# Attention scores of two heads in two 64-row halves of TensorE, in one visit a unit around the products with v

## The chip, the core and the metric

The kernel runs on one core of one Trainium2 chip. The core has TensorE (PE; its weight loads are shown apart as PEld), VectorE (DVE), ScalarE (ACT), GpSimd (POOL) and SyncE (SP, here a queue that issues DMAs). TensorE writes to PSUM, which holds eight banks of 512 float32 values for each of its 128 partitions. The metric is the time on the device in microseconds (us), the median of several runs.

## The reference, cut to what matters

The kernel computes a transformer block: an adaptive layer norm, attention with a memory over four segments, its output projection with residual, a second norm, and a gated feed-forward network. The change is in the attention of a segment:

```python
B, S, D, H = 1, 2048, 576, 32
Dh = D // H; N = 4; L = S // N                 # head size 18, four segments of 512 positions
mask = (ar[:, None] < ar[None, :]) * (-1e9)
for s in range(N):
    qs, ks, vs = q[:, :, s], k[:, :, s], v[:, :, s]
    logits = jnp.einsum("bhqd,bhkd->bhqk", qs, ks) * scale + mask
    p = _softmax(logits, axis=-1)
    a_dot = jnp.einsum("bhqk,bhkd->bhqd", p, vs)
    a_mem = num / den                          # from the memory of the segments before
    o = g * a_mem + (1.0 - g) * a_dot
```

## The kernel before

The work goes in stages: the first norm with the projections to q, k and v (to about 227 us), the attention (to about 573 us), the feed-forward network (the rest). q and k lie in DRAM (`qD`, `kD`), split into a high and a low part, so that a product of three parts (high with high, low with high, high with low) has nearly the precision of float32. A head has 18 features, hence 54 rows of such parts.

The attention goes over 32 *units*: four heads of one segment each (`units`, `NU`). The four heads are two pairs (`a`), and a pair lies in one *stack*: 108 rows, 54 for each of its heads (`e`). In `kst` the rows of both heads hold k; in `qst` there is a column block for each head in which the other head's rows are zero, so a product over 108 rows gives one head's scores. Rows 108 and 109 hold ones in `kst` and the negated row maximum, high and low part, in `qst`, so that the products for the softmax (`p2_step`, 110 rows) come with the maximum subtracted. There are `NB` = 4 stacks. At any time unit u is in its scores and products with v, u + 1 waits for its maxima, u + 2 has its row maxima taken, and u + 3 is loaded.

For unit u the loop over steps k does, mixed with one another:
- `p1_step` for unit u + 2: scores of row block i (128 rows of q against the 128(i+1) keys that the mask leaves), in 3 PSUM banks (`S1B`, tag s1), and the maximum of each row by VectorE. Behind block 0 GpSimd splits the maxima into high and low (`mc`).
- event `m` for unit u + 1: TensorE transposes `mc` into `pmt`; event `n`: ScalarE copies it to `mr` (`mt_b`), and `put_m` writes it into the stack by DMA.
- `p2_step` for unit u: scores transposed (key block j against the queries that may see it), in 3 banks (`S2B`, tag s2), the exponential by ScalarE into `Pt`, and the diagonal block cut by GpSimd (`affine_select`).
- `av_step` for unit u - 1: the products of `Pt` with v, four heads in four groups of 32 columns of the array, all at step `BK` = 0, behind the first score product; then `ev_step` copies `av` on ScalarE.
- events `U` and `V`: `load_k` and `load_q` for unit u + 3. Other events are the output projection of the segment before (M, X, R, S, T), the memory terms (A, B, C, D, G), the second norm (l, p, x) and preparations of weights.

The order on every engine is the order of the code (`manual_schedule`): the table `PAT` says at which of the 11 steps of a unit each event stands, by the unit's half of a segment and parity, and `KP`, `RL` and `step_of` place further work by numbers of steps. All loads, `put_m` and stores of this stage are issued by SyncE's queue in that order. An instruction that waits holds up all that stand behind it on its engine.

Of the kernel before, what the change touches and what calls it, by code (L numbers as in the profile page):

```python
# [26 lines left out]
VC = 624  # L27
EPS = 1e-5
# [20 lines left out]
KP = (7, 8, 1, 3)  # L49
# [12 lines left out]
NE = 2  # L62
E1 = 2
E2 = 1
BK = 0
PAT = (["E", "", "m U D", "c", "n V G", "Q d", "M0", "g M1 M2 M3 X", "h A0", "R S q T Y Z B0", "A1 f P z B1 C"],
# [7 lines left out]
RL = (-10, -1, 0, 4, 4, 9, 10, 10, 12, 10, 11, 12, 15, 16)  # L74
SUMS = ((4, 3, 2, ALU.add), (5, 4, 0, ALU.subtract), (3, 0, 3, ALU.subtract), (6, 1, 5, ALU.subtract))
S1B, S2B, XB, WB = 3, 3, 2, 1
# [7 lines left out]
def block(ctx: ExitStack, tc: tile.TileContext, x, wqk, wv, wo, beta, wgu, wgr, wd, c, crow, w_mod, w_mod0, w_mod1, w_modc, xt, out):  # L84
# [58 lines left out]
    def new_stack(b, stk):  # L143
# [5 lines left out]
        nc.gpsimd.memset(f32(qst[b][:, 2:4]), 0.0)  # L149

    def new_ones(b):
        nc.sync.dma_start(f32(kst[b][108:110]).rearrange("p a (b c) -> p (a b) c", c=P),
                          ones[0:2, :].unsqueeze(1).to_broadcast([2, 8, P]))
# [36 lines left out]
    def load_k(u, b):  # L190
        s, q = units[u]
        k = kD[s].rearrange("(Q a f) z t -> Q f z a t", Q=8, a=2)[q]
        ks = f32(kst[b][0:108]).rearrange("(f z) a t -> f z a t", z=3)
        for z in range(3):
            nc.sync.dma_start(ks[:, z], k[:, z // 2])

    def load_q(u, b):
        s, q = units[u]
        v = qD[s].rearrange("f z t -> (f z) t").rearrange("(Q a r) t -> Q r a t", Q=8, a=2)[q]
        for r0, r1 in ((0, 48), (54, 102), (48, 54), (102, 108)):  # L200
            nc.sync.dma_start(f32(qst[b][r0:r1, r0 // 54:4:2, :]), v[r0:r1])

    def put_m(u, b):
        mr = mrow.pop(u)
        for a in range(2):
            nc.sync.dma_start(f32(qst[b][108 + a:109 + a]).rearrange("p a t -> p (a t)"), mr[16 * a:16 * a + 16])

    def p1_step(u, b, i, ps, jp, jb):
        if i == 3:
            mcol[u] = (mwk.tile([P, 4, 4], F32, tag="mx", name="mx"),  # L210
                       mwk.tile([P, 2, 4, 4], F32R, tag="mc", name="mc"))
        mx, mc = mcol[u]
        n = 128 * (i + 1)
        per = L // n if n <= 256 else 1
        for h0 in range(0, 4, per):
            bank = ps.tile([P, L], F32, tag="s1", name="s1", bufs=SB[-1])
# [1614 lines left out]
```

## Time and profile before

| | us |
|---|---|
| median of 3 runs | 1820.09 |
| lowest, highest | 1817.81, 1820.72 |
| profiled execution (its span) | 1819.8 |
| attention, 237.05 to 540.70 us (28 units) | 303.65 |
| TensorE busy in it | 295.98 |
| VectorE busy in it | 253.67 |
| ScalarE busy in it | 241.84 |
| GpSimd busy in it | 204.06 |

The profile gives no time for the profiled execution but its span, from the first to the last instruction. It comes from one execution on the chip. A timeline row has start, duration, engine, line of the kernel, operation, tile written <- tiles read, shape, the number of instructions merged into it, and in brackets the idle time ahead of it with what ended it. "108*128 108x512" is a product over 108 rows with 128 columns of weights and 512 columns streamed. SPq is the queue of SyncE: a row there is the issue of DMAs, not their transfer. Records of matmuls overlap, since they are pipelined, so what one costs is read from start to start.

### The profile page before, as it was taken

Reading aid. Unit: us, or ns where it says so; the run is one execution under the profiler, and the core shown is the slowest. Engines: PE = TensorE matmul, PEld = TensorE weight load, DVE = VectorE, ACT = ScalarE, POOL = GpSimd, SP = SyncE. Lnnn points to the kernel's source line nnn. Section 1 sums busy time; section 2 is a strip of 40 time slices with the busy share of each in tenths; the row PEclk is TensorE's granted clock in tenths of the full one; section 3 lists DMA queues with packets and bytes.
Section 4 is the critical chain, followed back from the end, with each engine's and each line's share of the span. In section 5 each row is a group of like instructions: output and inputs, shape, how many; then the busy total and the mean of one; then the engine's idle time right before and its main releaser. Section 6 shows DMA issues by size and latency. Waiting matters only on the chain.

```text
span 1819.8 us, 31453 instructions
## 1 busy us (share of the span) xinstructions
PE 1791.3 (98%) x10627; PEld 1521.3 (84%) x10627; DVE 1484.4 (82%) x3365; ACT 1086.4 (60%) x2374; POOL 674.9 (37%) x1110
## 2 busy tenths in 40 slices
PE   7999989999999999999999999999999999999999
PEld 4888856777777888888888888888888888888888
DVE  7556378888886899889889889868888888888886
ACT  4334288878776567777777777534544544444542
POOL 3444077775567655656656656300000000000000
PEclk9999999999999999999999999999999999999999
DMA  7768765667657655455455354494233334324331
GB/s 264 265 225 278 263 208 178 214 201 220 172 170 237 202 178 185 135 181 178 134 183 176 115 173 147 158 311 151 101 107 121 98 96 130 104 82 129 107 103 53
DMA packets 146115, 306.26 MB, mean 168 GB/s; under 512 B 30916, under 2 KB 61764, under 8 KB 144164
## 3 DMA queue, kind: packets, MB, share of 16 engines
q1 hardware_dynamic: 134772, 260.19, 46.7%
q10 hardware_dynamic: 11184, 44.07, 6.1%
q8 instruction: 85, 1.39, 0.3%
q14 instruction: 74, 0.61, 0.1%
HBM read 198.69 MB, written 104.94 MB: 167 GB/s over the span
## 4 chain that ended last, share of the span: by engine, by line
PE 93%; DMA 2%; ACT 2%; DVE 1%; issue 1%; POOL 0%; SPq 0%; ACTq 0%; DVEq 0%; POOLq 0%
PE A L1349 25%; PE pd L1468 20%; PE C L1349 13%; PE B L1349 6%; PE pp L113 5%; PE s L218 4%; PE av L745 4%; PE s L721 3%; PE pv L113 3%; PE pw L863 3%; PE pd L1488 3%; ACT Pt L728 1%; PE pn L931 1%; PE pm L550 1%; PE px L766 1%
## 5 line engine op out<-in xcount | busy, mean ns | idle before, releaser
L1349 PE MATMUL A<-y,wh 128*128 128x512 f32 x1152 | 404.1, 391 | 0.7 <-ACT cu L1378 0.7
L1476 DVE TENSOR_TENSOR acc<-acc,pd 128x576 f32<-128x576 f32 x327 | 245.2, 750 | 78.2 <-PE pd L1468 71.9
L1468 PE MATMUL pd<-dh,ah 128*128 128x288 f32 x896 | 267.4, 298 | 0.0
L1468 PE MATMUL pd<-dl,ah 128*128 128x288 f32 x896 | 263.8, 294 | 0.0
L1468 PE MATMUL pd<-dh,al 128*128 128x288 f32 x896 | 262.4, 293 | 0.0
L223 DVE CUSTOM_DVE_ANT_0 junk<-s,tri 128x512 bf16<-128x512 f32 (+1 forms) x480 | 207.3, 484 | 58.0 <-PE s L218 44.2
L1349 PEld LDWEIGHTS A<-y,wh 128*128 128x128 f32 x1152 | 216.2, 188 | 39.2 <-ACT cu L1378 1.1
L1310 DVE TENSOR_TENSOR wl<-O,wh 128x256 fp32r<-128x256 f32 x504 | 240.2, 480 | 1.5 <-ACT wh L1309 0.9
L1349 PE MATMUL A<-y,wl 128*128 128x512 f32 x576 | 224.5, 390 | 0.0
L728 ACT ACTIVATE Pt<-s 128x512 f32<-128x512 f32 (+1 forms) x352 | 182.3, 558 | 46.1 <-PE s L721 28.3
L1349 PE MATMUL C<-y,wh 128*128 128x512 f32 x576 | 202.7, 393 | 0.0
L1309 ACT CAST wh<-O 128x256 fp32r<-128x256 f32 x504 | 198.2, 405 | 2.0 <-POOL O L1303 1.7
L1468 PEld LDWEIGHTS pd<-dh,ah 128*128 128x128 f32 x896 | 168.1, 188 | 18.5 <-ACT pd L1444 3.9
L1468 PEld LDWEIGHTS pd<-dl,ah 128*128 128x128 f32 x896 | 169.5, 189 | 16.2
L1414 DVE TENSOR_TENSOR al<-sg,ah 128x512 fp32r<-128x512 f32 x240 | 177.5, 740 | 6.7 <-ACT ah L1413 6.4
L1303 POOL TENSOR_TENSOR O<-O 128x128 f32<-128x128 f32 x280 | 155.2, 587 | 72.2 <-DMA O<-in_wgu_dram 39.8
L1468 PEld LDWEIGHTS pd<-dh,al 128*128 128x128 f32 x896 | 169.1, 189 | 0.0
L1413 ACT CAST ah<-sg 128x512 fp32r<-128x512 f32 x240 | 149.1, 621 | 25.6 <-DVE sg L1373 25.1
L1349 PEld LDWEIGHTS C<-y,wh 128*128 128x128 f32 x576 | 108.0, 188 | 18.7
L1349 PEld LDWEIGHTS A<-y,wl 128*128 128x128 f32 x576 | 108.2, 188 | 14.9
L1349 PE MATMUL A<-y,wr 128*128 128x512 f32 x288 | 113.6, 394 | 0.0
L1349 PE MATMUL C<-y,wl 128*128 128x512 f32 x288 | 112.1, 389 | 0.0
(400 smaller groups left out, 4144.4 us busy)
## 6 DMA issues: line engine op xcount, KB each, us to landing
wr<-rD SPq DMA_DIRECT2D x216, 112.0 KB
O<-in_wgu_dram SPq DMA_DIRECT2D x36, 512.0 KB
oD<-O ACTq DMA_DIRECT2D x36, 512.0 KB
O<-oD SPq DMA_DIRECT2D x36, 512.0 KB
O<-in_wgu_dram SPq DMA_DIRECT2D x36, 384.0 KB
y<-yD SPq DMA_DIRECT2D x11, 1024.0 KB
ks<-kD SPq DMA_DIRECT2D x72, 144.0 KB
kD<-fh SPq DMA_DIRECT2D x16, 512.0 KB
```

What stands on the lines that cost most here:

```text
L113: nc.tensor.matmul(ps, lhsT=a, rhs=b, start=(k == 0), stop=(k == 13))
L218: nc.tensor.matmul(bank[:, n * (h - h0):n * (h - h0) + n], lhsT=qst[b][0:108, h, 128 * i:128 * i + 128], rhs=kst[b][0:108, h // 2, 0:n], s ...
L223: nc.vector.tensor_tensor_reduce(junk[:, :n], bank[:, n * (h - h0):n * (h - h0) + n], tri[:, L - n:], 1.0, -3e38, op0=ALU.add, op1=ALU.max ...
L728: nc.scalar.activation(pt[:, h:h + per, :n], bank[:, :n * per].rearrange("p (a b) -> p a b", a=per), AF.Exp, scale=SCALE)
L1303: eng.tensor_tensor(o[:, d, i, s_], o[:, a, i, s_], o[:, b, i, s_], op=op)
L1309: nc.scalar.copy(wh, o)
L1310: later.append(lambda: nc.vector.tensor_tensor(wl, o, f32(wh), op=ALU.subtract))
L1349: nc.tensor.matmul(bank, lhsT=a, rhs=b, start=(first and n == 0), stop=(n == 6), skip_group_check=not first)
L1413: nc.scalar.copy(ah, src)
L1414: later.append(lambda: nc.vector.tensor_tensor(al, src, f32(ah), op=ALU.subtract))
L1468: nc.tensor.matmul(pd[:, i, :288], lhsT=a[:, tk], rhs=w, start=(add and k == 0), stop=(k == 2), skip_group_check=not add)
L1476: nc.vector.tensor_tensor(o, o, pd[:, :, :288], op=ALU.add)
```

## The change

Each stack gets its two heads into two halves of the array's rows: head e of a pair in rows 64e to 64e + 53, its maxima (ones in `kst`) in the two rows behind. A product over the rows of one half uses a tile of 64 rows and 128 columns, and the two heads of a pair are issued one behind the other into different banks. The products done so are those of row blocks 3, 2 and 0 for the maxima (`p1_pair`) and of key block 0 for the softmax (`p2_pair`). They stand together around `av`: ahead of it the two pairs of row block 3 for unit u + 2 and one pair of scores of unit u; behind it the other pair of scores and the pairs of row blocks 2 and 0. The rest (row block 1 by `p1_full`, key blocks 1 to 3 by `p2_step`) is computed on all rows of the same stacks: 118 rows (`K1`) or 120 (`K2`), with zeros in the other half of `qst`. Since rows 54 and 55 of a stack hold maxima of the unit before, `load_q` writes zeros there first.

A unit has 9 steps (`NI`) instead of 11. The maxima on VectorE are put into a list (`tq`), from which `max_step` takes as many as `TTRS` says at a step. The banks become 4 for the maxima and 2 for the scores. `load_k` issues six DMAs instead of three, `load_q` five instead of four, `put_m` four instead of two; `affine_select` is issued for each pair in key block 0.

```diff
+KR = 3 * DH
+K1 = 64 + KR
+K2 = K1 + 2
...
-KP = (7, 8, 1, 3)
+KP = (8, 3, 1, 1)
...
-BK = 0
-PAT = (["E", "", "m U D", "c", "n V G", "Q d", "M0", "g M1 M2 M3 X", "h A0", "R S q T Y Z B0", "A1 f P z B1 C"],
...
+PAT = (["D U g", "m G", "c n h Q", "d V", "q M0", "M1", "M2 Y", "M3 X Z", "z R S T f P"],
...
+NI = len(PAT[0])
+TTRS = (0, 2, 2, 2, 2, 0, 2, 2, 0)
+S1F = (4, 5)
...
-S1B, S2B, XB, WB = 3, 3, 2, 1
+S1B, S2B, XB, WB = 4, 2, 2, 1
...
+        nc.vector.memset(f32(kst[b][32:64]), 0.0)
...
     def load_k(u, b):
         s, q = units[u]
-        k = kD[s].rearrange("(Q a f) z t -> Q f z a t", Q=8, a=2)[q]
-        ks = f32(kst[b][0:108]).rearrange("(f z) a t -> f z a t", z=3)
-        for z in range(3):
-            nc.sync.dma_start(ks[:, z], k[:, z // 2])
+        k = kD[s].rearrange("(Q a e f) z t -> Q e f z a t", Q=8, a=2, e=2)[q]
+        for e in range(2):
+            ks = f32(kst[b][64 * e:64 * e + KR]).rearrange("(f z) a t -> f z a t", z=3)
+            for z in range(3):
+                nc.sync.dma_start(ks[:, z], k[e][:, z // 2])
 
     def load_q(u, b):
         s, q = units[u]
         v = qD[s].rearrange("f z t -> (f z) t").rearrange("(Q a r) t -> Q r a t", Q=8, a=2)[q]
-        for r0, r1 in ((0, 48), (54, 102), (48, 54), (102, 108)):
-            nc.sync.dma_start(f32(qst[b][r0:r1, r0 // 54:4:2, :]), v[r0:r1])
+        for e in range(2):
+            for r0, r1 in ((0, 48), (48, KR)):
+                nc.sync.dma_start(f32(qst[b][64 * e + r0:64 * e + r1, 2 * e:2 * e + 2, :]), v[KR * e + r0:KR * e + r1])
+        nc.sync.dma_start(f32(qst[b][KR:KR + 2, 0:2, :]), tri[P - 1:P, :].unsqueeze(1).to_broadcast([1, 4, L]))
 
     def put_m(u, b):
         mr = mrow.pop(u)
-        for a in range(2):
-            nc.sync.dma_start(f32(qst[b][108 + a:109 + a]).rearrange("p a t -> p (a t)"), mr[16 * a:16 * a + 16])
-
-    def p1_step(u, b, i, ps, jp, jb):
+        for e in range(2):
+            for z in range(2):
+                r = 64 * e + KR + z
+                nc.sync.dma_start(f32(qst[b][r:r + 1, 2 * e:2 * e + 2, :]).rearrange("p a t -> p (a t)"),
+                                  mr[16 * z + 8 * e:16 * z + 8 * e + 8])
...
+    def row_max(u, bank, o, h, i, jp):
+        n = 128 * (i + 1)
+        junk = jp.tile([P, L], BF16, tag="junk", name="junk", bufs=1) if jp else xw[:, 2000:2256].bitcast(BF16)
+        nc.vector.tensor_tensor_reduce(junk[:, :n], bank[:, o:o + n], tri[:, L - n:], 1.0, -3e38,
+                                       op0=ALU.add, op1=ALU.max, accum_out=mcol[u][0][:, h % 2, h // 2, i:i + 1])
+
+    def p1_full(u, b, i, h0, per, ps):
+        n = 128 * (i + 1)
+        bank = ps.tile([P, L], F32, tag="s1", name="s1", bufs=SB[-1])
+        for h in range(h0, h0 + per):
+            nc.tensor.matmul(bank[:, n * (h - h0):n * (h - h0) + n], lhsT=qst[b][0:K1, 2 * (h % 2) + h // 2, 128 * i:128 * i + 128],
+                             rhs=kst[b][0:K1, h // 2, 0:n], start=True, stop=True)
+        return [(bank, n * (h - h0), h, i) for h in range(h0, h0 + per)]
...
+    tq = []
+
+    def max_step(n):
+        for _ in range(min(n, len(tq))):
+            f = tq.pop(0)
+            f()
+
+    def p1_list(u, ts):
+        for t in ts:
+            tq.append(lambda t=t: row_max(u, *t, wk))
+
+    def p1_pair(u, a, ii):
+        if not NE <= u < NU:
+            return
+        if a == 0 and 3 in ii:
+            new_mx(u)
+        b = u % NB
+        banks = [ps.tile([P, L], F32, tag="s1", name="s1", bufs=S1B) for _ in range(2)]
+        o, ts = 0, [[], []]
+        for i in ii:
+            n = 128 * (i + 1)
+            for e in range(2):
+                r = slice(64 * e, 64 * e + KR)
+                nc.tensor.matmul(banks[e][:, o:o + n], lhsT=qst[b][r, 2 * e + a, 128 * i:128 * i + 128],
+                                 rhs=kst[b][r, a, 0:n], start=True, stop=True)
+                ts[e].append((banks[e], o, 2 * a + e, i))
+            o += n
+        p1_list(u, ts[0] + ts[1])
+
+    def p1_rest(u, a):
+        if not NE <= u < NU:
+            return
+        p1_list(u, p1_full(u, u % NB, 1, 2 * a, 2, ps))
+        if a == 1:
+            tq.append(lambda: p1_done(u))
...
+    def bank2(u):
+        nb2[0] += 1
+        s2 = u < NU - 2 or nb2[0] % 4 < 2
+        return ps.tile([P, L], F32, tag="s2" if s2 else "s1", name="s2", bufs=S2B if s2 else S1B)
+
+    def keep(v, n):
+        nc.gpsimd.affine_select(out=v, in_=v, pattern=[[0, n], [1, P]], compare_op=ALU.is_ge,
+                                fill=0.0, base=0, channel_multiplier=-1)
+
+    def p2_pair(u, a):
+        if u >= NU:
+            return None
+        b = u % NB
+        banks = [bank2(u) for _ in range(2)]
+        for e in range(2):
+            r = slice(64 * e, 64 * e + KR + 2)
+            nc.tensor.matmul(banks[e], lhsT=kst[b][r, a, 0:128], rhs=qst[b][r, 2 * e + a, :], start=True, stop=True)
+        return banks
+
+    def p2_exp(u, a, banks):
+        if u >= NU:
+            return
+        pt = Pt[u, 0, a] = pp_.tile([P, 2, L], F32, tag=f"P0{a}", name="Pt", bufs=2 - a)
+        for e in range(2):
+            nc.scalar.activation(pt[:, e], banks[e], AF.Exp, scale=SCALE)
+        keep(pt[:, :, :P], 2)
...
-            ga = chain(*[p2_step(u, j) for j in range(4)])
-            gb = p1_seq(u + 2)
-            for k in range(11):
-                next(ga, None)
-                if k == BK and u:
-                    for j in range(4):
-                        av_step(u - 1, j)
-                next(ga, None)
-                next(gb, None)
-                if u == 0 and k == 0:
-                    stage_r()
-                if u == 17 and k == 0:
-                    stage_a()
-                if u == 24 and k == 0:
-                    stage_b()
-                if (u, k) in ((29, 2), (30, 5)):
+            ga = chain(*[p2_step(u, j) for j in range(1, 4)])
+            if u == 0:
+                stage_r()
+            if u == 17:
+                stage_a()
+            if u == 24:
+                stage_b()
+            for k in range(NI):
+                if k == 0:
+                    max_step(99)
+                    p1_pair(u + 2, 0, (3,))
+                    bk = p2_pair(u, 0)
+                    max_step(2)
+                    p1_pair(u + 2, 1, (3,))
+                    p2_exp(u, 0, bk)
+                    max_step(2)
+                elif k == 1:
+                    if u:
+                        for j in range(4):
+                            av_step(u - 1, j)
+                        ev_step(u - 1)
+                    bk = p2_pair(u, 1)
+                    for a in range(2):
+                        p1_pair(u + 2, a, (2, 0))
+                    p2_exp(u, 1, bk)
+                else:
+                    next(ga, None)
+                    if k in S1F:
+                        p1_rest(u + 2, S1F.index(k))
+                    next(ga, None)
+                if (u, k) in ((29, 1), (30, 4)):
                     load_y(0, u - 29)
-                if u in (29, 30) and k == 7:
+                if u in (29, 30) and k == 6:
                     load_x3(u - 29)
                 for ev in PAT[q // 4 * 2 + u % 2][k].split():
                     event(ev, u)
-                for f in sched.pop(11 * u + k, ()):
+                for f in sched.pop(NI * u + k, ()):
                     f()
-                if k == 5 and 3 <= q < 7 and s < 3:
+                if k:
+                    max_step(TTRS[k])
```

On TensorE, around the products with v of one unit, this stood before (L218 is a product for maxima of unit u + 2, L721 one for scores of unit u, L745 `av` of unit u - 1, L238 the transpose of the maxima of unit u + 1):

```order
L721 MATMUL s_2953<-qs_92,ks_93 128x256 x2
L218 MATMUL s_2959<-y_77 128x128 x4
L721 MATMUL s_2983<-qs_2502,ks_2503 128x512
L745 MATMUL av<-Pt,vq_2507 32x512 x4
L745 MATMUL av<-Pt,vq_2507 32x384 x4
L745 MATMUL av<-Pt,vq_2507 32x256 x4
L745 MATMUL av<-Pt,vq_2507 32x128 x4
L218 MATMUL s_3006<-ks_89,y_77 128x512
L721 MATMUL s_3016<-qs_2502,ks_2503 128x512
L218 MATMUL s_3019<-ks_89,y_77 128x512
L721 MATMUL s_3028<-qs_2502,ks_2503 128x512
```

One score product stood ahead of `av` and the first product for maxima behind it. And now on TensorE (L748 is `p1_pair`, L785 `p2_pair`, L833 `av`):

```order
L748 MATMUL s_3028<-ks_90,y_77 128x512
L748 MATMUL s_3029<-ks_90,y_77 128x512
L785 MATMUL s_3032<-qs_2524,ks_2525 128x512
L785 MATMUL s_3033<-qs_2524,ks_2525 128x512
L748 MATMUL s_3040<-ks_90,y_77 128x512
L748 MATMUL s_3041<-ks_90,y_77 128x512
L833 MATMUL av<-Pt,vq_2531 32x512 x4
L833 MATMUL av<-Pt,vq_2531 32x384 x4
L833 MATMUL av<-Pt,vq_2531 32x256 x4
L833 MATMUL av<-Pt,vq_2531 32x128 x4
L785 MATMUL s_3083<-qs_2524,ks_2525 128x512
L785 MATMUL s_3084<-qs_2524,ks_2525 128x512
```

The first thing of the visit is now the pair for maxima on the stack that was loaded last. Six products stand ahead of `av`, where one stood.

On SyncE one unit's DMAs stood before as follows (L206 is `put_m` of unit u + 1, L201 `load_q` and L195 `load_k` of unit u + 3, the others stores and loads of other work):

```order
L206 DMA qs_92<-mr 1x16x128 x2
L201 DMA y_77<-qD_108 48x2x512 x2
L201 DMA y_77<-qD_108 6x2x512 x2
L1170 DMA rD_0_211<-yh_2484 128x896
L1171 DMA rD_1_212<-yh_2484 128x896
L195 DMA ks_89<-kD_112 36x2x512 x3
L206 DMA qs_2502<-mr 1x16x128 x2
L201 DMA y_77<-qD_108 48x2x512 x2
```

And now on SyncE (L218 is `put_m`, L210 and L211 `load_q`, L203 `load_k`):

```order
L218 DMA y_77<-mr 1x8x128 x4
L210 DMA qs_2524<-qD_112 48x2x512
L210 DMA qs_2524<-qD_112 6x2x512
L210 DMA qs_2524<-qD_112 48x2x512
L210 DMA qs_2524<-qD_112 6x2x512
L211 DMA qs_2524<-tri 2x2x512
L958 DMA xD_148<-xr 128x576
L910 DMA xr<-in_x_dram 128x576
L993 DMA qf<-qF_121 126x512
L203 DMA y_77<-kD_116 18x2x512 x6
```

`load_q` is still behind `put_m`, which has four DMAs now, and the second head's rows come behind all of the first's.

On ScalarE, from the copy of `av` (L757) to that of the maxima (L242), it was

```order
L757 COPY avs<-av 128x512
L728 ACTIVATE Pt<-s_4247 128x512
L728 ACTIVATE Pt<-s_4254 128x512
L728 ACTIVATE Pt<-s_4266 128x512
L728 ACTIVATE Pt<-s_4279 128x384
L242 COPY mr<-pmt 32x128
```

and is now on ScalarE (L845 the copy of `av`, L793 and L813 exponentials, L268 the maxima):

```order
L845 COPY avs<-av 128x512
L793 ACTIVATE Pt<-s_5608 128x512
L793 ACTIVATE Pt<-s_5609 128x512
L813 ACTIVATE Pt<-s_5636 128x384
L268 COPY mr<-pmt 32x128
```

The copy of the maxima has two exponentials of the second pair and one of key block 1 ahead of it in place of three of key block 0 and one of key block 1.

More of the change, by code (lines that the diff above doesn't have):

```diff
@@ L227, in p1_step @@
         if i == 0:
[L228 to L232 removed]
+            p1_done(u)
         yield
@@ L731, in p2_step @@
                 yield
[L732 to L733 removed]
+        keep(pt[:, :, :P], 4)
         yield
```

84 lines of the change are left out of this document (40 added, 44 removed), and 6 rows, old and new, of the table PAT.

## The prediction

> **What bounds the kernel now.** I read the busy shares first, then the stage of the change by windows, then that stage's timeline on TensorE, ScalarE and the issuing queue of SyncE, and last its waits.
>
> ```profile
> span 1819.8 us, 31453 instructions
> 237.00:540.60 303.60, 16.42 (x28) 0.99 0.65 196
> 237.05:540.70 303.65, 295.98 (x2318) 223.09 (x2317) 253.67 (x1075) 241.84 (x530) 204.06 (x374) 0.99 0.65 196
> 237.05 1.39 PE L745 MATMUL av<-Pt,vq 128*32 128x512 f32 x12
> 540.70 1.07 PE L745 MATMUL av<-Pt,vq 128*32 128x512 f32 x8
> ```
>
> The second row is a window cut to the copies of `av` alone (L757): 28 of them, one a unit. The third is the same stretch for TensorE, its weight loads, VectorE, ScalarE and GpSimd. So 28 units of attention take 303.65 us, 10.84 us each, from one start of the products with v to the next. TensorE is busy for 295.98 us of them; VectorE has 253.67/28 = 9.06 us of work a unit, ScalarE 8.64, GpSimd 7.29. The granted clock is 0.99, so the clock is not the subject. A unit looks like this on TensorE (line, tile, shape; the number ahead is the start):
>
> ```profile
> 321.46 0.40 PE L218 MATMUL s<-ks,qs 108*128 108x512 f32 x1
> 321.70 0.40 PE L721 MATMUL s<-y,ks 110*128 110x512 f32 x1
> 325.12 0.34 PE L218 MATMUL s<-ks,qs 108*128 108x384 f32 x1
> 325.30 0.34 PE L721 MATMUL s<-y,ks 110*128 110x384 f32 x1
> 327.63 0.56 PE L218 MATMUL s<-ks,qs 108*128 108x128 f32 x4
> 328.03 0.45 PE L721 MATMUL s<-qs,ks 110*128 110x512 f32 x1
> 328.41 2.36 PE L745 MATMUL av<-Pt,vq 128*32 128x512 f32 x32
> 330.70 0.49 PE L218 MATMUL s<-y 108*128 108x512 f32 x1
> 331.03 0.40 PE L721 MATMUL s<-qs,ks 110*128 110x512 f32 x1
> ```
>
> From start to start a score product of 512 columns costs 0.24 us, one of 384 0.18, four of 128 columns 0.40. The last product ahead of `av` holds TensorE 0.38 us instead of 0.24 (0.14 for the change to 32-column groups), `av` takes 2.29, and the first one behind it 0.33 instead of 0.24 (0.09 for the way back). TensorE carries the stage, and that is what the change attacks. But another chain runs through the same unit:
>
> ```profile
> 321.01 0.59 ACT L757 COPY avs<-av 128x512 f32<-128x512 f32 x1 [0.70 <-PE av L745]
> 321.66 0.60 ACT L728 ACTIVATE Pt<-s 128x512 f32<-128x512 f32 x1
> 322.42 1.47 ACT L728 ACTIVATE Pt<-s 128x512 f32<-128x512 f32 x3
> 323.76 0.24 ACT L242 COPY mr<-pmt 32x128 f32<-32x128 f32 x1
> 326.47 2.05 ACT L728 ACTIVATE Pt<-s 128x384 f32<-128x384 f32 x4 [0.28 <-PE s L721]
> 330.83 0.58 ACT L757 COPY avs<-av 128x512 f32<-128x512 f32 x1
> 317.44 2.52 SPq L195 DMA_DIRECT2D y<-kD  x3
> 324.02 1.21 SPq L206 DMA_DIRECT2D qs<-mr  x2
> 325.27 1.78 SPq L201 DMA_DIRECT2D y<-qD  x4
> ```
>
> The copy of the maxima `mr` stands on ScalarE behind the copy of `av` and some exponentials. SyncE issues the two DMAs of `put_m` 0.26 us after `mr` starts, and only behind them, in the same queue, the four of `load_q` for the unit that comes three later. That order is also in the code before, and it hurts little, because the loaded stack is first read by the row-maximum product that stands behind the next `av`: the load was issued at 325.27 and the product ran at 330.70. How long such a load takes is seen in a unit where TensorE had to wait for it:
>
> ```profile
> 423.49 1.22 SPq L206 DMA_DIRECT2D qs<-mr  x2
> 424.75 1.76 SPq L201 DMA_DIRECT2D y<-qD  x4
> 426.24 0.47 PE L721 MATMUL s<-qs,ks 110*128 110x512 f32 x1 [0.33 <-DMA qs<-mr]
> 428.96 0.19 PEld L218 LDWEIGHTS s<-ks,y 108*128 108x128 f32 x1 [0.23 <-DMA y<-qD]
> ```
>
> Issued from 424.75, landed when the weight load goes at 428.96: 4.21 us. That load was due behind `av` and was 0.23 us late.
>
> **The change part by part.** *Pairs in halves.* Four products of 512 columns for the row maxima (row block 3), four of 512 for the scores of key block 0, four of 384 (row block 2) and four of 128 (row block 0) become two pairs each, one head in rows 0 to 63, the other in rows 64 to 127. No row of this trace shows a product on 64 rows with a partner on the other 64. The nearest is `av`: its products with v run in four 32-column groups. Of the two bounds, a pair for the price of one product or of two, I take the first by that row, since there too the small tiles of one array go together. Then 512 columns save 2 x 0.24 for each of two sets, 0.96. For the other two sets the weights limit: four products of 128 columns in 0.40 us are 0.10 us for one load, 0.20 for a pair's two. 384 columns: 4 x 0.175 = 0.70 become 2 x 0.20 = 0.40, saving 0.30; 128 columns: 0.40 stay 0.40. Together 1.26 us a unit. The visit has two changes of array mode more than now; by the 0.14 and 0.09 above they cost 0 to 0.23. TensorE's own work falls by 1.03 to 1.26 us a unit, or by -0.23 to 0 if halves do not overlap. The price of an overlapped pair is only on a page: the Trainium skill, TensorEngine Tiling (Array Packing), section Theoretical Speedup, gives up to 2x for contractions of 64 rows or fewer; by it the saving is the 1.26 us, and no run here shows it yet.
>
> *Order of the visit.* The row-maximum pair of the unit two ahead becomes the first thing of a unit, ahead of `av`, and `put_m` has four DMAs instead of two, all still ahead of `load_q`. So the stack must have landed 3.15 us earlier than now: behind the load come three pairs of 0.24 (0.72), the change of mode (0.14) and `av` (2.29). This closes a loop over one unit that TensorE cannot shorten:
> - visit to the end of `av`: 3.15 us;
> - to the first `put_m`: `avs` starts 0.13 us after `av` (in the unit above 330.70 against 330.83 on ScalarE), then 0.65 to the first exponential (321.01 to 321.66), two of 512 columns at 1.47/3 = 0.49, one of 384 at 2.05/4 = 0.51, then `mr` and 0.26 to the issue: 0.13 + 0.65 + 0.98 + 0.51 + 0.26 = 2.53;
> - four `put_m` DMAs. Two take 325.27 - 324.02 = 1.25 us now, 0.62 each, with 16 pieces of 512 bytes; the new ones have 8. The cheapest stack load bounds them below:
>
> ```profile
> L201 SPq DMA_DIRECT2D qs<-qD x64: 258/341/690, 154.1 to 538.0; - x64
> ```
>
>   0.26 to 0.62 us each; I take 0.50, nearer to the row of the same transfer: 2.0 (1.04 to 2.48);
> - `load_q`, first issue to landed: 4.21.
>
> The loop is 3.15 + 2.53 + 2.0 + 4.21 = 11.9 us, between 10.93 and 12.37, against 10.84 now. TensorE's shorter work then buys only idle time ahead of each visit. On the load the Trainium skill, DMA: Bandwidth & Descriptors, section Anatomy of one DMA — SWDGE (gpsimd) path, puts a DMA at 2.0 us plus its bytes over 436 GB/s. By an estimate from that page the last of the four would land some 3.5 us after the first issue, and the loop would be 11.2 us, 1829 in all; but it is measured on another path than SyncE's, and the row above says 4.21.
>
> *The other edits, costed at nothing.* `load_k` goes from three DMAs to six of half the size, and `load_q` gains one of zeros. Three take 2.52 us now; six take 1.6 (0.26 each) to 5.0. They stand ahead of `put_m` and can start at the visit, and the first `put_m` is 3.15 + 2.53 = 5.68 us away; that cover is thin when other stores share the queue, and where it is gone, each us late is a us of the loop. The zeros stand behind the four loads, and are first needed by row block 1, in the middle of the next unit. The row maxima keep their 16 instructions on VectorE, now with the four longest under `av`; the selects become five on GpSimd, two of them of half the size, and the work of both fits an 11.9 us unit. Score banks go from three to two, maximum banks from three to four: the six steps behind the visit have one bank each, over 1 us apart, and an exponential has 0.49, so I put 0 on it (an upper bound of 0.3 us a unit would be an exponential that comes one half late).
>
> *Sum.* 28 units of 11.9 are 333.2 us, 29.5 more than 303.65. The last three units have no row maxima and no load; two score pairs save 0.48 less two changes of mode, 0.25 each: -0.8. The stages before and behind have the same work, and the one behind starts later by as much: 1819.8 + 29.5 - 0.8 = 1848.5. The median of the runs is 1820.09, 0.3 above the profiled execution: 1849.
>
> **The rivals.** *The halves win.* If the load lands in time, a unit falls by TensorE's 1.03 us to 9.8, still above VectorE's 9.06: 28 x 1.03 = 29 us, 1791; if half of it is lost to waits between engines, 1805. For it speak TensorE's share, and these waits between 281 and 560 us (in total, times, longest), in which VectorE and ScalarE idle for want of score products around `av`, which four pairs ahead of `av` would feed:
>
> ```profile
> ACT Pt L728 <- PE s L721: 26.3, 40, 1.8
> DVE junk L223 <- PE s L218: 21.2, 21, 2.2
> ```
>
> Against it speaks the loop. It decides at 10.84 us: the part on SyncE would have to be 10.84 - 5.68 = 5.16 us, where the rows give 6.2, and 5.25 with all four `put_m` at their least.
>
> *The two cancel.* With a loop of 10.71 to 10.97 us the whole is within 0.2% (3.6 us over 28 units, about what a measurement of this kernel can tell from no change). Only the lowest end of the bounds reaches it.
>
> *The halves do not overlap.* Then the visit has 3 x 0.24 = 0.72 us more, and `mr` comes about 0.25 later, since its transpose and one exponential wait for 0.24 + 0.30 more of products: 12.9 us a unit, 28 x 2.03 = 57, 1876. Only the absence of any such row speaks for it, and `av` against it.
>
> **How the numbers follow.** The loop of SyncE and ScalarE: 0.66, 1822 (10.93 us a unit) to 1862 (12.37), likeliest 1849. The halves win: 0.21, 1791 to 1812. They cancel: 0.07. No overlap: 0.06, about 1876. Faster is 0.21, the same 0.08 with the low end of the loop, slower 0.71. Since cases of both signs hold much, the range goes from 1800, which leaves out half of the winning case, to 1866, which leaves out the last: about 0.17 outside. The likeliest case's own range is 1822 to 1862.
>
> **What would show it.** In the profile after: TensorE idle of 1 to 3 us ahead of the first pair of nearly each unit, released by a DMA into the stack from `qD`; units near 11.9 us even early in the stage, where they are shortest now; VectorE and ScalarE less busy than 0.83 and 0.80 of the stage; four `put_m` issues taking about 2.0 us and the loads starting 4.5 us behind the end of `av`. The pairs' second product should end within hundredths of the first, and two pairs of 512 columns should be 0.24 us apart. The prediction is wrong if the first pair starts without a wait: then either the loads land much sooner than 4.21 us or `mr` is copied earlier than 2.3 us behind `av`.

## The result, and the profile after

The changed kernel takes 1968.81 us (median of 4 runs, 1967.01 to 1970.89) against 1820.4 us before: ratio 1.0821, 95% interval 1.0807 to 1.0834. It is 148 us slower; 29 were forecast, and 1866 was the upper end of the range. Of the two runs of the kernel e4 below, one was slow (6100 us, for a reason that its record does not show), and e4's time is that of the other.

The busy shares, the clock row of the 40 slices, and the stage of the attention by windows (the columns are start and end, length, then busy time and count of TensorE, its weight loads, VectorE, ScalarE and GpSimd, granted clock, share of the DMA engines, GB/s):

```profile
span 1969.1 us, 31862 instructions
PE 1835.8 (93%) x10627; PEld 1520.5 (77%) x10627; DVE 1534.7 (78%) x3369; ACT 1090.9 (55%) x2374; POOL 678.6 (34%) x1142
PEclk9989977889889899999999999999999999999999
261.56:688.93 427.37, 332.10 (x2318) 218.41 (x2317) 294.90 (x1084) 245.00 (x525) 208.24 (x403) 0.87 0.47 138
```

The span grew by 149.3 us, in three pieces. The first `av` starts at 261.56 instead of 237.05: 24.5 us are lost before a single unit is done. The next 28 intervals take 427.37 instead of 303.65 us: 123.7 us, 15.26 a unit instead of 10.84. What follows has 1280.2 us instead of 1279.1. TensorE waits for 95 us of the 28 units (427.37 - 332.10), and what it does takes 36 us longer, at a granted clock of 0.87. Of its waits, 34 us are for `qD` (27 waits) and another 34 us are score products that wait for exponentials. One early unit on TensorE, then on ScalarE and on SyncE's queue:

```profile
349.49 0.50 PE L805 MATMUL s<-qs,ks 120*128 120x256 f32 x2 [0.45 <-ACT Pt L813]
352.53 0.47 PE L748 MATMUL s<-ks,y 54*128 54x512 f32 x1 [2.54 <-DMA y<-qD]
353.53 0.76 PE L748 MATMUL s<-ks,y 54*128 54x512 f32 x1 [0.53 <-DMA y<-qD]
353.67 1.05 PE L785 MATMUL s<-qs,ks 56*128 56x512 f32 x2
354.23 0.92 PE L748 MATMUL s<-ks,y 54*128 54x512 f32 x2
355.08 4.49 PE L833 MATMUL av<-Pt,vq 128*32 128x512 f32 x32
359.50 0.62 PE L785 MATMUL s<-qs,ks 56*128 56x512 f32 x2
```

```profile
359.64 0.59 ACT L845 COPY avs<-av 128x512 f32<-128x512 f32 x1 [4.09 <-PE av L833]
361.77 0.24 ACT L268 COPY mr<-pmt 32x128 f32<-32x128 f32 x1
351.62 4.78 SPq L203 DMA_DIRECT2D ks<-kD  x6
362.03 2.72 SPq L218 DMA_DIRECT2D y<-mr  x4
364.79 1.53 SPq L210 DMA_DIRECT2D qs<-qD  x4
366.37 0.70 SPq L211 DMA_DIRECT2D qs<-tri  x1
368.82 3.43 SPq L203 DMA_DIRECT2D ks<-kD  x4
```

The wait of 2.54 us for the stack's load, released by `qD`, is the one forecast, and so is its loop: `av` ends at 359.50, `put_m` is issued 2.53 us later, the load behind it. But the visit (from 353.53 to the end of `av`) takes 5.97 us instead of 3.15, since the clock has fallen to half:

```profile
350.00:352.40 2.40, 0.00 (x0) 0.00 (x0) 1.35 (x8) 1.47 (x5) 2.05 (x4) 1.00 0.77 190
355.10:359.40 4.30, 4.30 (x33) 1.36 (x32) 1.67 (x5) 0.45 (x1) 1.03 (x2) 0.50 0.46 128
```

TensorE does nothing in the first window, at a clock of 1.00, and is busy all through the second at 0.50.

### The profile page after: what moved, and what is told of

It reads as the page before. It is cut to its first block, busy times and chain, and to the rows that moved or that the text cites. A ratio compares the mean times of both kernels' runs of the same rounds, so it can differ in the third digit from the quotient of the medians.

```text
span 1969.1 us, 31862 instructions
## 1 busy us (share of the span) xinstructions
PE 1835.8 (93%) x10627; PEld 1520.5 (77%) x10627; DVE 1534.7 (78%) x3369; ACT 1090.9 (55%) x2374; POOL 678.6 (34%) x1142
## 4 chain that ended last, share of the span: by engine, by line
PE 79%; DMA 7%; SPq 4%; ACT 4%; DVE 3%; issue 2%; POOL 1%; ACTq 0%; DVEq 0%; POOLq 0%
PE A L1435 23%; PE pd L1554 18%; PE C L1435 12%; PE B L1435 6%; PE pp L118 5%; PE pv L118 3%; PE av L833 3%; SPq L218 2%; PE pd L1574 2%; DMA qf<-qF 2%; PE pw L951 2%; DMA y<-qD 1%; SPq L210 1%; PE s L748 1%; DMA qs<-qD 1%
## 5 line engine op out<-in xcount | busy, mean ns | idle before, releaser
L228 DVE CUSTOM_DVE_ANT_0 junk<-s,tri 128x512 bf16<-128x512 f32 (+1 forms) x480 | 235.2, 490 | 111.1 <-PE s L748 80.4
L775 POOL TENSOR_SCALAR_AFFINE_SELECT Pt<-Pt 128x512 f32<-128x512 f32 (+1 forms) x160 | 87.4, 551 | 216.2 <-ACT Pt L793 172.7
L813 ACT ACTIVATE Pt<-s 128x384 f32<-128x384 f32 (+1 forms) x224 | 117.0, 538 | 37.0 <-PE s L805 34.3
```

The costliest lines, as they stand in the source:

```text
L228: nc.vector.tensor_tensor_reduce(junk[:, :n], bank[:, o:o + n], tri[:, L - n:], 1.0, -3e38, op0=ALU.add, op1=ALU.max, accum_out=mcol[u][0] ...
L775: nc.gpsimd.affine_select(out=v, in_=v, pattern=[[0, n], [1, P]], compare_op=ALU.is_ge, fill=0.0, base=0, channel_multiplier=-1)
L813: nc.scalar.activation(pt[:, h:h + per, :n], bank[:, :n * per].rearrange("p (a b) -> p a b", a=per), AF.Exp, scale=SCALE)
```

## The experiments

The theories: Q, SyncE's queue closes a loop over the unit; C, the granted clock makes it worse; S, two score banks instead of three cost; E, the early loads delay the start; R, products on half the rows do not hold the clock; V, ScalarE idles while `av` runs; against them H, the halves and their changes of mode are slow themselves. "First `av`" and "28 units" are read as above. Times are medians; the kernel before had 1817.7 to 1819.3 beside these runs.

| kernel | us | ratio to before | first `av` at | 28 units | clock there |
|---|---|---|---|---|---|
| before | 1820 | 1 | 237.1 | 303.7 | 0.99 |
| changed | 1969 | 1.082 | 261.6 | 427.4 | 0.87 |
| load first (e1) | 1931 | 1.061 (1.058 to 1.064) | 263.8 | 382.9 | 0.90 |
| fillers, 54 rows (e2) | 1991 | 1.095 (1.088 to 1.101) | 268.7 | 445.4 | 0.89 |
| full rows (e3) | 1998 | 1.098 (1.094 to 1.103) | 263.3 | 454.1 | 0.86 |
| few DMAs (e4) | 1931 (one run) | 1.061 | 258.7 | 390.5 | 0.89 |
| short queue (e5) | 1903 | 1.046 (1.045 to 1.048) | 262.2 | 357.6 | 0.93 |
| short queue, full rows (e6) | 1908 | 1.049 (1.047 to 1.050) | 265.9 | 360.5 | 0.96 |
| fillers, 118 rows (e7) | 1972 | 1.084 (1.082 to 1.087) | 265.4 | 425.1 | 0.96 |
| short queue, 3 and 3 banks (e8) | 1940 | 1.067 (1.065 to 1.069) | 259.5 | 400.2 | 0.92 |
| early loads elsewhere (e9) | 1948 | 1.071 (1.070 to 1.073) | 244.2 | 420.0 | 0.88 |
| e5 and e9 together (e10) | 1896 | 1.043 (1.041 to 1.045) | 254.8 | 356.8 | 0.93 |
| before, 4 and 2 banks (e11) | 1834 | 1.009 (1.007 to 1.010) | 238.7 | 316.1 | 0.99 |
| before, more DMAs (e12) | 1863 | 1.024 (1.022 to 1.026) | 237.5 | 339.9 | 0.99 |
| order of before, new stacks (e13) | 1831 | 1.007 (1.005 to 1.009) | 250.0 | 304.9 | 0.99 |
| e13 with a pair on each side (e14) | 1837 | 1.010 (1.009 to 1.012) | 246.3 | 305.7 | 1.00 |
| e10, scores ahead of `av` (e16) | 1923 | 1.057 (1.055 to 1.059) | 255.4 | 381.9 | 0.92 |

**e1, the load ahead of `put_m`.**

```diff
-PAT = (["D U g", ... "d V", ...
+PAT = (["D U V g", ... "d", ...
```

> The changed kernel with load_q issued right behind load_k, ahead of put_m. Theory Q (SyncE's queue closes the loop: 11.3 us of issues a unit, the stack's load behind put_m): the wait for qD ahead of the visit goes, but put_m now stands behind 7.1 us of loads, lands some 12 us behind the start of av, and the second pair of the next visit waits for it; units fall from 15 to 13 or 14, in all 1915 to 1945 us. Theory H (the pairs in halves, their changes of mode and the two score banks make TensorE's own unit long): nothing changes, 1960 to 1975.

1931 us, 38 less, as theory Q has it; H falls. No wait of TensorE for `qD` is among the longer ones left in the stage, and `put_m` is now what comes late.

**e2 and e7, fillers.** Ahead of each visit, in `p1_pair`, into the bank that the pair then overwrites; e7 has `0:K1` (118 rows) where e2 has `0:KR` (54):

```diff
+            for _ in range(12):
+                nc.tensor.matmul(banks[0], lhsT=kst[(u - 1) % NB][0:KR, 0, 0:128],
+                                 rhs=kst[(u - 1) % NB][0:KR, 0, :], start=True, stop=True)
```

> The changed kernel with 12 extra products of 512 columns (54 rows, about 2.9 us at full clock) ahead of each visit's first pair, on a stack that landed a unit before, into the bank that the pair then overwrites. Theory C (the idle time ahead of the visit lowers TensorE's granted clock and so doubles the time of the visit): the clock of the stage rises from 0.87 to over 0.95, av takes 2.4 us instead of 3.0 to 4.5, and the units get 1 to 2 us shorter although TensorE has more work: 1910 to 1945 us. Without C: the fillers only fill the wait or lengthen it, 1969 to 2050.

> The changed kernel with the 12 extra products as in the filler run, but on 118 rows instead of 54. In the filler run the granted clock fell to 0.5 while TensorE was busy with the fillers. Theory R (the clock follows how much of the array works, so products on 54 rows count as half idle): the clock stays at 1.0 through fillers and visit, av takes 2.1 us from first to last start in all units, stage clock over 0.95, 1930 to 1965 us. Theory T (only time without any product counts, and the fall in the filler run had another cause): the same as with 54 rows, av at 3 to 4 us in the first ten units, 1980 to 2000 us.

With 54 rows the clock falls although TensorE hardly pauses. The same visit of the run with 54 rows, then that with 118 (its fillers start at 321.76):

```profile
328.19 3.01 PE L745 MATMUL s<-ks 54*128 54x512 f32 x12
333.30 3.24 PE L837 MATMUL av<-Pt,vq 128*32 128x512 f32 x32
328.20:331.00 2.80, 2.80 (x13) 2.31 (x13) 1.53 (x8) 1.53 (x5) 2.35 (x6) 1.00 0.78 177
332.00:335.00 3.00, 3.00 (x13) 1.05 (x17) 2.32 (x9) 1.08 (x2) 1.16 (x2) 0.50 0.53 165
```

```profile
321.76 2.93 PE L745 MATMUL s<-ks 118*128 118x512 f32 x12
325.52 2.36 PE L837 MATMUL av<-Pt,vq 128*32 128x512 f32 x32
321.50:324.20 2.70, 2.70 (x13) 2.26 (x14) 1.79 (x9) 1.90 (x6) 2.15 (x5) 1.00 0.76 184
325.00:328.00 3.00, 3.00 (x40) 1.28 (x38) 2.41 (x7) 1.14 (x3) 1.45 (x2) 1.00 0.43 130
```

The row of `av` is 2.36 us at full clock. In the unit shown with 54 rows TensorE paused once between fillers and `av`, for 0.33 us. In the next one it worked from the fillers (from 342.98) to `av` (347.85) without a pause, and the clock fell as well:

```profile
344.00:345.00 1.00, 1.00 (x6) 0.80 (x5) 0.87 (x4) 0.00 (x0) 0.94 (x2) 1.00 0.71 180
346.00:347.00 1.00, 1.00 (x6) 0.91 (x6) 0.06 (x1) 0.00 (x0) 0.00 (x0) 0.50 1.03 401
```

With 118 rows the 32 products of `av` have the full-clock pace in all of the first 28 units; with 54 rows in none of the first ten. Both runs issue the same number of products with the same columns, so theory R stands: in these ten units products on 54 rows did not hold the clock, products on 118 did. The ten took 155.6 us in the changed kernel, 156.1 with the fillers on 54 rows and 144.7 with those on 118: the full clock is worth 1.1 us a unit there. In three of them (numbers 4 to 6, counted from 0) the gain was larger, 15.75, 15.20 and 15.29 us against 12.83, 12.74 and 12.93, with 2.9 us of useless work in each. But the whole run, 1972 us, missed the 1930 to 1965 expected: in most later units the clock was full anyway, and there the fillers only cost. The filler run with 54 rows missed the range of theory C and came out in the one given for its absence; theory C was incomplete, since it asked for work without asking how much of the array works.

On the clock the Trainium skill, TensorE: Matmul & The Clock Gate, section Part 1: The HAM clock gate, says that TensorE drops to half rate after an idle window of about 3.4 us and comes back after a busy one, and gives this gate no state in between. The 0.50 and 1.00 above agree. So does the length of the low stretch in the unit shown of the changed kernel, 352.95 to 359.78, which is two such windows; but in the 3.41 us ahead of it TensorE was idle for only 2.53 us. It ties the state to whether TensorE is busy; here it was, and the clock fell, so by this measurement the rows in use count too.

**e3, pairs on all rows.**

```diff
-                nc.tensor.matmul(banks[e][:, o:o + n], lhsT=qst[b][r, 2 * e + a, ...], rhs=kst[b][r, a, 0:n], ...
+                nc.tensor.matmul(banks[e][:, o:o + n], lhsT=qst[b][0:K1, 2 * e + a, ...], rhs=kst[b][0:K1, a, 0:n], ...
```

and the same in `p2_pair` with `K2`.

> The changed kernel, same order and DMAs, but each product of a pair on all rows of the stack (118 or 120) instead of a half. Theory Q with halves that run side by side: the visit has 0.72 us more ahead of the end of av, more at a low clock, and this lies in the loop: units 0.7 to 1.2 us longer, 1988 to 2003 us. Theory H: the changes of mode go and nothing is lost, 1940 to 1970.

1998 us: 29 more, 0.95 us a unit. Halves are worth what was said while they stand in the loop; H falls.

**e4, e5, e6, e8: a short queue.** e4 keeps `kD` in three rows a feature, so that a stack's load is two plain blocks of rows a half, and lays the maxima out so that a half's two rows come from 16 rows of `mr`:

```diff
-            for z in range(3):
-                nc.sync.dma_start(ks[:, z], k[e][:, z // 2])
+            for r0, r1 in ((0, 48), (48, KR)):
+                nc.sync.dma_start(f32(kst[b][64 * e + r0:64 * e + r1]), v[e][r0:r1])
...
-            for z in range(2):
-                r = 64 * e + KR + z
-                nc.sync.dma_start(f32(qst[b][r:r + 1, ...
+            r = 64 * e + KR
+            nc.sync.dma_start(f32(qst[b][r:r + 2, ... mr[16 * e:16 * e + 16])
```

> The changed kernel in its order, with kD kept in three rows a feature as qD is, so that load_k takes four DMAs like load_q (about 1.5 us instead of 4.6), and the maxima laid out so that put_m takes two DMAs instead of four (1.2 us instead of 2.6). Theory Q: SyncE's issues fall from 11.3 to about 7 us a unit, the loop to about 11 us, the waits ahead of the visit to about 1 us, the clock comes back to 0.97 or more, and the delay ahead of the first unit shrinks by some 5 to 15 us: 1835 to 1870 us in all. Theory H: units stay at 14 to 15 us, 1940 to 1970.

1931 us, outside both ranges. The load still stood behind `put_m`, and behind that a second wait showed: `qf`, loaded last in a unit and read first in the next, now came late and held ScalarE, and with it `mr`. So e5 issues `load_q` and the load of `qf` right behind `load_k` (`"D U V f g"`); e6 is e5 with full rows; e8 is e5 with `S1B, S2B = 3, 3`.

> The kernel with few DMAs (load_k four, put_m two), with load_q and the load of qf issued right behind load_k, ahead of put_m. Theory Q (SyncE's queue is what is left): put_m starts as soon as mr is copied, the loads land 8 us ahead of their use, ScalarE no longer waits for qf; no wait of TensorE for a DMA is left at the visit, the clock of the stage is 0.97 or more, units of 10.0 to 10.8 us, 1815 to 1845 us in all. Theory S (two score banks instead of three and a low clock in units with little TensorE work bound it as well): units stay at 11.5 to 13 us with waits of TensorE for exponentials, 1860 to 1905 us.

> The kernel with the short queue, each product of a pair on all rows instead of a half. If a pair of halves costs one product (my step): 1.0 to 1.3 us a unit more of TensorE's time; where TensorE bounds, 28 to 36 us above the short queue with halves, less where other engines do. If halves don't overlap: no difference, or up to 7 us faster by the changes of mode left out.

> The kernel with the short queue and three banks each for maxima and scores, instead of four and two. Theory S: the scores wait for exponentials less, units 0.3 to 1 us shorter, 8 to 30 us faster than the short queue. Theory Q: within 5 us of it, or slower, since the four maximum products of a visit now wait for a bank.

e5: 1903 us, 66 less than the changed kernel, and TensorE waits for no DMA at the visit any more. But units of 12.8 us are theory S's, not Q's. Among what is left are waits of the scores for exponentials (total, times, longest), of weight loads and of products, which can overlap:

```profile
PEld s L804 <- ACT Pt L812: 30.3, 34, 2.5
PE s L804 <- ACT Pt L812: 20.8, 17, 2.2
```

A third score bank at the price of a maximum bank (e8) is no cure: 37 us slower than e5, since the pairs of maxima then wait for VectorE. And e6 shows what the halves gain where the queue is short: 3 us of 28 units (360.5 against 357.6). In e5 TensorE is busy for 310.94 us at 0.93, in e6 for 322.59 at 0.96; part of what the halves save comes back as a lower clock, and the rest is idle time.

One edit of the change stands in no experiment by itself. `junk`, the tile that takes the unused output of a row maximum, has one buffer in the changed kernel (`bufs=1` in `row_max`), where the kernel before gave it four. Two maxima of 512 columns then start 0.84 us apart (the first two rows, from e5) instead of 0.61 (the other two, from before):

```profile
542.65 0.69 DVE L226 CUSTOM_DVE_ANT_0 junk<-s,tri 128x512 bf16<-128x512 f32 x1
543.49 0.69 DVE L226 CUSTOM_DVE_ANT_0 junk<-s,tri 128x512 bf16<-128x512 f32 x1
```

```profile
322.04 0.69 DVE L223 CUSTOM_DVE_ANT_0 junk<-s,tri 128x512 bf16<-128x512 f32 x1
322.65 0.69 DVE L223 CUSTOM_DVE_ANT_0 junk<-s,tri 128x512 bf16<-128x512 f32 x1
```

The median is 0.84 in every kernel with one buffer and 0.61 in every kernel with four. VectorE is busy for 290.05 us of e5's 28 units instead of 253.67, and in the chain of work that ended last in them the maxima hold 21.5%, more than any other line, where they held 2.8% before. So VectorE holds back the units of e5 too, beside the exponentials; no run changes the buffers alone, and what they cost is open.

**e9 and e10, the early loads.**

```diff
-                nc.sync.dma_start(ks[:, z], k[e][:, z // 2])
+                (nc.scalar if u < 3 else nc.sync).dma_start(ks[:, z], k[e][:, z // 2])
...
-        nc.sync.dma_start(f32(qst[b][KR:KR + 2, 0:2, :]), tri ...
+        if u >= NB:
+            nc.sync.dma_start(f32(qst[b][KR:KR + 2, 0:2, :]), tri ...
```

and `new_ones` on ScalarE's queue.

> The changed kernel, with the first three stacks' load_k and the rows of ones issued from ScalarE's queue instead of SyncE's, and the zeros of load_q left out for the first four stacks (their memory is zero already). Units are as in the changed kernel. Theory E (18.7 us are lost ahead of the first unit because the first stacks' loads stand behind more DMAs on SyncE, so that the row maxima of units 0 and 1 land in a bunch on TensorE, each waiting for VectorE, instead of between projection products): the first av starts at 240 to 248 us instead of 261.6, 1945 to 1958 us in all. If the bunch has another cause: 1963 to 1973.

> The kernel with the short queue, and with the early loads changed in the same way. Theory E and theory Q add up: 1903 less 12 to 20, so 1883 to 1891 us; with units of 12.5 us as in the short queue. If the early loss is made good later by fuller units: 1895 to 1905.

In the projection stage a scheduler sets the order, by when it thinks operands land. In the changed kernel the maxima of unit 0 therefore stand on TensorE in a bunch, behind the projection instead of between its products, each waiting for VectorE, and the transpose of the maxima behind them for GpSimd:

```profile
99.47 0.44 PE L235 MATMUL s<-y 118*128 118x384 f32 x1 [0.35 <-DVE mx L228]
104.00 1.11 PE L235 MATMUL s<-y 118*128 118x128 f32 x4 [0.20 <-DVE mx L228]
108.79 0.40 PE L264 MATMUL pmt<-ident,mc 128*32 128x128 f32 x1 [3.68 <-POOL mc L245]
```

With the early loads elsewhere the first `av` is at 244.2 instead of 261.6, and the whole is 21 us faster: theory E. Which of the DMAs taken off the queue moves the order is not settled; e12, with thirteen early DMAs of `load_k` and `put_m` more than before, starts its first unit on time. In e10 the two remedies add up only in part: 7 us on top of e5, where 12 to 20 were expected.

**e11 and e12, one part of the change alone, in the kernel before.** e11: `S1B, S2B = 4, 2`. e12:

```diff
-            nc.sync.dma_start(ks[:, z], k[:, z // 2])
+            for a in range(2):
+                nc.sync.dma_start(ks[:, z, a], k[:, z // 2, a])
...
+            for h in range(2):
+                nc.sync.dma_start(f32(qst[b][108 + a:109 + a, 2 * h:2 * h + 2])..., mr[16 * a + 8 * h:16 * a + 8 * h + 8])
```

> The kernel before, with four banks for the maxima and two for the scores instead of three and three. Theory S (two score banks cost): 0.3 to 1.0 us a unit by waits of TensorE for exponentials, 1828 to 1850 us. My step (banks at nothing): within 4 us of 1819.

> The kernel before, with the DMAs of load_k cut into six and those of put_m into four, as in the changed kernel, and nothing else. Theory Q in its plain form (the count of issues on SyncE decides): units 0.5 to 2 us longer, 1833 to 1875 us. Theory Q with the loop (the count costs only because the load's first reader now stands at the front of the next unit): the loads come later but stay hidden, 1817 to 1829 us.

Four and two banks alone cost 16 us, and the waits for exponentials, of weight loads and products together, grow from 1.9 to 36.7 us (of e11 two rows, against 0.9 and 1.0 before):

```profile
PEld s L721 <- ACT Pt L728: 29.3, 74, 1.7
PE s L721 <- ACT Pt L728: 7.4, 14, 1.4
```

Nothing but more DMAs, of the same bytes, costs 45 us, a surprise: the loop was thought to need the new order. The queue of e12 shows that it doesn't. It runs from one load into the next, and TensorE waits at the end of it, here for the product behind `av`:

```profile
400.50 4.56 SPq L196 DMA_DIRECT2D ks<-kD  x6
405.16 2.66 SPq L208 DMA_DIRECT2D y<-mr  x4
407.86 1.63 SPq L202 DMA_DIRECT2D qs<-qD  x4
412.68 0.47 PE L221 MATMUL s<-ks,qs 108*128 108x512 f32 x1 [0.79 <-DMA qs<-qD]
```

**e13, e14, e16.** e13 has the steps, the banks, the interleaving and the four buffers of `junk` of the kernel before on the new stacks, with the few DMAs of e4 (the loads at their old steps) and the early loads on ScalarE; all products on all rows. e14 adds one pair of halves ahead of `av` (scores) and one behind it (maxima). e16 is e10 with `p2_pair(u, 1)` moved ahead of `av`.

> The order of the kernel before (its steps, its three and three banks, no pairs) on the stacks of the change, with the short queue and the early loads on ScalarE's queue; every product on all rows. If the loss is made of the order, the banks and the DMAs: 1812 to 1828 us, like before. If the stacks themselves cost (118 rows instead of 108, zeros, masks): 1835 to 1865 us.

> As the kernel with the order of before on the new stacks, but the two score products ahead of each av and the two 512-column maximum products behind it are pairs in halves: one pair on each side of av. Halves side by side save 0.48 us a unit of TensorE's time less at most 0.23 for changes of mode, 7 to 13 us in all, and the result is under the kernel before, 1803 to 1815 us. If what products on half the rows do to the clock, or the second bank held at once, eats it: within 4 us of its parent, or up to 15 us slower.

> The kernel with the short queue and the early loads (1896 us), with the second pair of scores issued ahead of av instead of behind it, so that ScalarE has two more exponentials while av runs. Theory V (what is left is ScalarE idle under the visit, 1.6 us a unit in waits for av, and TensorE idle for exponentials later): units 0.3 to 1.0 us shorter, 1868 to 1888 us. Rival (with two banks the second pair only waits for the first pair's exponentials, now ahead of av): within 5 us of 1896, or slower.

e13 gives the units back: 304.87 us for 28, against 303.65 before. Its 13 us more lie nearly all ahead of the first `av` (249.98 against 237.05), where `kD` has 20 more stores; whether these cause it was not tested. So the stacks cost nothing in the units, and what e10 lacks there, 52 us, is the order with its banks and the single buffer of `junk`, which no run separates. In e10 the row maxima hold 23.3% of the chain that ended last in the units, in e13 3.5%. e14 is no faster than e13, and 1.0% slower than before. One pair costs there (its first product, then the next one on all rows), against two single products of e13:

```profile
328.66 0.50 PE L766 MATMUL s<-ks,qs 54*128 54x512 f32 x2
329.09 0.50 PE L825 MATMUL s<-y,ks 120*128 120x512 f32 x1
```

```profile
334.82 0.50 PE L232 MATMUL s<-ks,qs 118*128 118x512 f32 x1
335.16 0.40 PE L808 MATMUL s<-y,ks 120*128 120x512 f32 x1
335.39 0.39 PE L232 MATMUL s<-ks,qs 118*128 118x512 f32 x1
```

0.43 us for the pair with its way back to all rows, 0.34 + 0.23 = 0.57 for two products: 0.14 saved, not 0.24, and TensorE's busy time over the units is the same in both (297.75 and 297.82). e16 is 26 us slower than e10: the second pair waits for the first pair's exponentials with `av` behind it. Theory V as a remedy falls. How the rest of the order's cost, some 40 us beside the 12.5 us that two banks cost in e11's units, divides among the clock, the wait for exponentials, the slower row maxima and the long visit is not settled.

## Why the prediction was wrong, step by step

- *Pairs in halves: right.* Both products start together and a pair takes the time of one. At full clock, in e5's visit, the second row is a pair in the 0.40 us of a single product of 512 columns, and the three starts are 0.33 (with a change of mode) and 0.24 apart:

```profile
541.18 0.50 PE L747 MATMUL s<-ks,y 54*128 54x512 f32 x2
541.51 0.40 PE L784 MATMUL s<-qs,ks 56*128 56x512 f32 x2
541.75 0.40 PE L747 MATMUL s<-ks,y 54*128 54x512 f32 x2
```

- *The loop over SyncE and ScalarE: right in kind, mis-sized.* In the unit shown above: `av` to `put_m` 2.53 us, as forecast; `put_m` 2.76 to the load instead of 2.0; the load 4.56 (from 364.79 until the next visit's second product, at 369.35) instead of 4.21; the visit 5.97 instead of 3.15. Together 15.8 against 11.9. The four DMAs of `put_m` went past the upper bound of 2.48: half the pieces, and no DMA cheaper.
- *"The clock is not the subject": wrong.* That sentence read the clock of the kernel before. The same text forecast 1 to 3 us of idle TensorE in each unit and sixteen products a unit on half the rows, and did not ask what these do to the clock. In the unit shown it is the largest term of the error, 2.8 us of the 3.9. Over all 28 units it is less: the two runs with fillers, which differ in the rows and so in the clock, are 20 us apart (445.4 and 425.1).
- *Six DMAs of `load_k` at nothing: wrong.* They take 4.78 us. The text had 5.0 as its upper end and called the cover thin, yet took 0 and left the cost out of the range; e12 prices this and `put_m` at 45 us even in the order before, more than the whole range above the forecast.
- *Two score banks at nothing: wrong*, 16 us in e11. The bound of 0.3 us a unit stood in the text, and neither the sum nor the range had it; e11's units lost 0.45.
- *VectorE's maxima as before: wrong.* The text counted 16 instructions a unit, saw that their work fits an 11.9 us unit, and did not ask about the buffers of `junk`. VectorE is busy for 10.5 us a unit (294.90/28) instead of 9.06, and its maxima head the chain in e5 and e10. What this adds to the changed kernel's time stays open. With 10.5 us on VectorE, the case in which the halves win at 9.8 us a unit was out of reach in this kernel.
- *"The stages before and behind have the same work": wrong for the one before*, by 24.5 us. It has the same products, but also the early loads, and its order of instructions is made from when these land. The change of the order was there to be read ahead of the run, in TensorE's sequence of the early maxima.
- *Sum and range.* Only the loop's ends were carried into the range; the costs of `load_k` and of the banks, put at nothing, were not, though the text had a bound for each. The rival with the longest time, no overlap, doubted the one price that came out right.
- *What would show it.* The waits of 1 to 3 us for `qD` ahead of the first pair came, VectorE and ScalarE fell to 0.69 and 0.57 of the stage, and the load starts 5.3 us behind `av` instead of 4.5; units near 11.9 did not come.

## What to carry to other kernels

Before a loop's length is added up, ask what its own idle time does to the clock, and carry every cost put at nothing into the range with its bound. Count the DMAs that a queue issues in a period, not their bytes: cutting the same bytes into more of them, 45 us, was the largest price found here for one edit alone. When a helper is rewritten, compare its buffers with the old one's before the time of its engine is taken over. Grouping products so that they fill one engine better pays only if that engine is still the limit in the new order, and the finished order of each stage should be read, the untouched ones too.

## What was not expected of the hardware

The clock follows how much of the array works, not only whether it works: 12 products on 54 rows, in 3.01 us at full clock, were followed by a clock of 0.50 in each of the first ten units, 12 on 118 rows in 2.93 us by 1.00.

The time that SyncE takes to issue a DMA hardly follows its size. The first row is `load_k` after (18 x 2 pieces of 2048 bytes each), the second before (36 x 2), the third `load_q`, which moves 48 x 2 or 6 x 2; the columns are shortest, median and longest in ns:

```profile
L203 SPq DMA_DIRECT2D ks<-kD x144: 737/746/1122, 84.7 to 677.1; - x144
```

```profile
L195 SPq DMA_DIRECT2D ks<-kD x72: 759/816/1441, 81.5 to 530.3; - x72
```

```profile
L210 SPq DMA_DIRECT2D qs<-qD x64: 307/326/1105, 172.5 to 685.3; - x64
L211 SPq DMA_DIRECT2D qs<-tri x16: 695/703/719, 174.1 to 685.7; - x16
```

Half the bytes saves 0.07 us of 0.82; a block of rows that lie side by side is issued in 0.33 us, rows three apart or the few zeros in 0.70 to 0.75.
